# Input rows of a long convolution in sixteen half-array products within one set, modulation vectors broadcast through DRAM, and the second group of channel parameters on GpSimd

## The chip, the cores and the metric

The kernel runs on one core of one Trainium2 chip. The metric is device time in microseconds (us) of a whole run; lower is better. The engines of a core are named as in the profile: PE (TensorE products; PEld its weight loads), DVE (VectorE), ACT (ScalarE), POOL (GpSimd) and SP (SyncE, which issues most DMAs). Each engine works through its own list of instructions in order and waits there on semaphores that other engines and DMAs raise.

## The reference

A block of 2048 tokens by 448 channels goes through two stages, each ahead of a layer norm that is scaled and shifted by vectors made from a condition `c`:

```python
mod = (silu(c) @ w_mod).reshape(1, 6, 1, 448)      # sa, ca, ga, sb, cb, gb
h = layernorm(x) * (1 + ca) + sa
x = x + ga * s4d(h, log_A_real, A_imag, C_real, C_imag, log_dt, D_skip)
h = layernorm(x) * (1 + cb) + sb
x = x + gb * token_mlp(h, w1, b1, w2, b2)          # two matmuls over the token axis, gelu
```

`s4d` makes for each of 448 channels a convolution kernel of 2048 taps, `K = 2 Re sum_n C_n exp(A_n dt l)` over 256 states, and convolves the channel with it (an FFT in the reference).

## The kernel before

The convolution is done as a product of two-step Fourier transforms of length 4096 = 32 x 64 split between PE and the elementwise engines. The program has three parts in a row: the making of `K` with the transform of the input beside it (to about 255 us and on to 380 us), the products and the inverse transform, and the token MLP, which is a stream of PE products to the end.

**Steps and windows.** `K` is made in 56 steps `s` of 16 channels by half of the states. A step (`st_step`) has six ACT functions on 128x512 (`Abs`, `Sin`), four DVE products `E` (L651 to L655) and two POOL products `G` (L649, L650), and PE turns `E` and `G` into `K` (`st_kgen`, `kg`, L676). POOL also makes `w` and `m` (`st_mag2`, L628 and L630), which `E` needs. The phases come from PE (`st_phase`, L601, tiles `xe` and `xg` of PSUM) out of small tiles `lph` that SP loads from `pars`, a table in DRAM. Every eight steps a window (`window(s)`, at s = 0, 8, 16 ...) makes the magnitudes `mag` of the next eight with `Exp` (L612), because ACT's tables for `Exp` and `Sin` have to be swapped; a window has eight parts `e`, and within each PE's products for the next magnitudes come ahead of whatever else PE has to do there.

**Parameters.** Channels come in four groups q of 128. For group 0, `first_chain` turns A, C and dt into logarithms and phases, before step 0, and sends rows to `lex`, `lph` and `pars`. For the groups 1 to 3 a generator (`chain(q)`) does the same with some 36 DVE operations on 128x256; it stops at "logs" until the next window has run `Ln`, `Arctan` and `Exp` for it on ACT. `more(n)` runs n of its steps at fixed places: `pace[s]` in a step, `WPACE` in a part of a window. Its `split` makes a pair `hl` (high and low part; three buffers) which SP stores to `pars`.

**Input side.** `x` (2048x448) is loaded into `xt` by POOL DMAs (`x_load`), DVE takes mean and variance of each of 16 rows of tiles (`u_stats`), `u_norm` normalises them, and `u_rows` does the 32-point step: PE products of `xt` with `wu` into a PSUM tile `pu` (pool `pms`, three buffers), then one DVE product with the vector `mod[1]` (L526) into `yt` (three buffers), then a store of 448 KB to `yu_d` in DRAM. `u_load` reads that back transposed (`yi`), and `u_cols` does the 64-point step, with results `uo` stored to `us_d`. The vectors `mod[0..5]` are made by `modulation(k)`: PE multiplies `w_mod` (loaded by `wm_load`) with a copy of silu(c) in 128 columns (`scb`), so that each result comes out on all 128 partitions, and ACT copies it.

**What sets the order.** PE, ACT, DVE and POOL run in the order in which the code is written: operations that read PSUM are put in the lists `dve` and `act` and emitted by `flush`. SP's order is written order up to step 8 (`first.close()`), and after that it is chosen at build time by a scheduler that knows estimated durations; on the chip SP then goes through that list in order. Each DMA also takes one of eight semaphores per kind of queue in turn, so a DMA is issued only when the one eight places earlier has landed.

Of the kernel before, what the change touches and what calls it, by code (L numbers as in the profile page):

```python
# [11 lines left out]
F32 = mybir.dt.float32  # L12
# [27 lines left out]
def dft_tables():  # L40
# [16 lines left out]
    t["WU"] = np.tile(w1.transpose(1, 2, 0).reshape(32, 64), (4, 1))  # L57
# [45 lines left out]
    t["S2"] = su.reshape(2, 4, 8, 2, 32 * P).transpose(3, 0, 2, 1, 4).reshape(P, 32 * P)  # L103
# [113 lines left out]
def tile_adaln_s4d_mixer(ctx, tc, i, out):  # L217
# [6 lines left out]
    yu_d = dram.tile([2, 32, 2, 8, 4, D], F32, name="yu_d")  # L224
    us_d = dram.tile([2, 32, P, DC], F32, name="us_d")
    v_d = dram.tile([32, P, D], F32, name="v_d")
    x2_d = dram.tile([L, D], F32, name="x2_d")

# [9 lines left out]
    with ExitStack() as es:  # L238
# [27 lines left out]
        def par_load(q):  # L266
            n = min(P, D - P * q)
            raws[q] = {}
            for nm in ("A_C_real", "A_C_imag", "A_log_A_real", "A_A_imag"):
                raws[q][nm] = qp.tile([P, N], F32, tag=nm, name=nm, bufs=2)  # L270
                nc.sync.dma_start(raws[q][nm][0:n], i[nm][P * q : P * q + n])
# [40 lines left out]
        wu = xp.tile([P, 64], F32, name="wu")  # L312
        wms = {}

        def wm_load(k, tile, eng=nc.sync):
            wms[k] = tile
            eng.dma_start(wms[k], i["w_mod"][:, k * D : (k + 1) * D].rearrange("(q p) d -> p q d", p=PP))
# [11 lines left out]
        def wm_slot(k):  # L329
            w = wm0.rearrange("p k d -> p (k d)")[0:PP]  # L330
            return w[:, 4 * D * (k % 4) : 4 * D * (k % 4 + 1)].rearrange("p (q d) -> p q d", q=4)

        late = {
            2: lambda: wm_load(2, wm_slot(2), G),
            3: lambda: wm_load(3, wm_slot(3), G),
            5: lambda: wm_load(0, wm_slot(0), G),
# [4 lines left out]
            9: lambda: nc.sync.dma_start(svt, i["SV"]),  # L343
            10: lambda: [s2_load(0), s2_load(1)],
            11: lambda: [s2_load(2), s2_load(3)],
            12: lambda: wm_load(4, xt[0:PP, 0:4]),
            13: lambda: wm_load(5, xt[0:PP, 4:8]),
# [14 lines left out]

        def chain(q):

# [7 lines left out]
            def split(src, places):  # L372
                hl = qp.tile([P, 2, N], F32R, tag="hl", name="hl", bufs=3)[0:n]
                V.tensor_copy(hl[:, 0], src)
                yield
                tt(hl[:, 1], src, hl[:, 0].bitcast(F32), ALU.subtract)
# [27 lines left out]
            stt(s, t, -80 * math.log(2.0) / 2.0**80, s, ALU.mult, ALU.add)  # L404
            yield
            stt(s, ya, 0.5, s, ALU.mult, ALU.add)
            yield
            ts(s, s, ldt2[0:n, q : q + 1], None, ALU.add)
# [4 lines left out]
            ts(ph, aim, dt4[0:n, q : q + 1], None, ALU.mult)  # L413
            yield
            ts(u, ph, MAGIC, MAGIC, ALU.add, ALU.subtract)
# [942 lines left out]
```

## Time and profile before

| | us |
|---|---|
| median of 3 runs | 725.6 |
| lowest and highest run | 722.94, 727.5 |
| the profiled execution, its own time | 724.45 |
| its span in the profile | 722.7 |
| PE busy in the span | 627.9 (87%) |
| DVE, ACT, POOL busy | 460.3, 438.7, 273.2 |
| granted PE clock, mean | 0.939 |

The page's line of 40 slices (18 us each) reads PE at 0 to 8 tenths in the first slices, between 7 and 9 up to 360 us, and at 9 or more from there to the end; DVE, ACT and POOL are busiest in the first half. A row of the timeline reads: start, duration, engine, line, operation, output<-input, and in brackets the idle time ahead of it on that engine and what ended it. A busy time is no measure of what an engine costs: what counts is whose work the others wait for in a stage.

### The profile page before, as it was taken

To read this page: it belongs to the slowest core of one execution; us is meant where nothing else is said; L and a number is where in the kernel's file an instruction comes from. 1 tells how busy PE (TensorE), PEld (TensorE's weight loads), DVE (VectorE), ACT (ScalarE), POOL (GpSimd) and SP (SyncE) were. 2 spreads that over 40 slices of the span, in tenths; PEclk is the share of its full clock that TensorE was granted. 3 is DMA by queue.
4 is the path that set the end of the run, shared out by engine and by line. 5 is a ranking of instruction groups with operands and counts; after the bars stand their busy time and mean duration, and the time that the engine had idled before them with its cause. 6 is when DMAs were issued, how large, how long until landed. Compare 5 with 4: busy or idle time off the path is not lost. (4 is left out here: it accounts for less than half of the span.)

```text
span 722.7 us, 18269 instructions
## 1 busy us (share of the span) xinstructions
PE 627.9 (87%) x7204; PEld 449.9 (62%) x7204; DVE 460.3 (64%) x891; ACT 438.7 (61%) x849; POOL 273.2 (38%) x342
## 2 busy tenths in 40 slices
PE   0769899969988877888778939999999999999997
PEld 0335344535535545555455607777999999999996
DVE  7579779689779667575776738777722263333441
ACT  5848578887988888979862339778622242222220
POOL 6487438438648867977865600000000000000000
PEclk9988857988999989899999969999999999999999
DMA  6795364277888644444325899993585436655540
GB/s 169 207 189 144 144 195 136 112 234 197 236 225 251 212 84 144 127 128 122 96 82 164 233 274 248 237 224 100 169 230 166 141 99 173 176 164 154 153 140 27
DMA packets 101636, 121.20 MB, mean 168 GB/s; under 512 B 13066, under 2 KB 87422, under 8 KB 101422
## 3 DMA queue, kind: packets, MB, share of 16 engines
q1 hardware_dynamic: 100014, 113.16, 55.4%
q0 software_dynamic: 1536, 6.87, 4.2%
q8 instruction: 57, 0.93, 0.6%
q14 instruction: 29, 0.24, 0.1%
HBM read 84.64 MB, written 34.87 MB: 165 GB/s over the span
## 5 line engine op out<-in xcount | busy, mean ns | idle before, releaser
L202 ACT CAST whi<-w 128x896 fp32r<-128x896 f32 x64 | 59.8, 938 | 135.2 <-PE o L1325 84.7
L649 POOL TENSOR_TENSOR G<-mag,gs 128x512 f32<-128x512 f32 x56 | 71.8, 1282 | 86.5 <-ACT gs L645 86.3
L211 DVE TENSOR_TENSOR wlo<-w,whi 128x896 fp32r<-128x896 f32 x64 | 68.1, 1087 | 43.9 <-ACT whi L202 31.5
L601 PE MATMUL xg<-tab,lph 64*128 64x512 f32 x112 | 68.3, 612 | 21.3 <-ACT xg L647 7.1
L1190 PE MATMUL acc<-h3h,whi 128*128 128x448 f32 x224 | 83.6, 373 | 0.1
L1191 PE MATMUL acc<-h3l,whi 128*128 128x448 f32 x224 | 82.1, 367 | 0.0
L1192 PE MATMUL acc<-h3h,wlo 128*128 128x448 f32 x224 | 81.3, 363 | 0.0
L1325 PE MATMUL o<-ul,whi 128*128 128x448 f32 x224 | 81.3, 363 | 0.0
L1324 PE MATMUL o<-uh,whi 128*128 128x448 f32 x224 | 81.2, 362 | 0.0
L1326 PE MATMUL o<-uh,wlo 128*128 128x448 f32 x224 | 80.6, 360 | 0.0
L601 PE MATMUL xe<-tab,lph 64*128 64x512 f32 x112 | 67.8, 607 | 12.4 <-ACT gs L646 7.0
L676 PEld LDWEIGHTS kg<-E,G 128*32 128x32 f32 x3584 | 57.9, 117 | 29.6 <-issue 14.9
L650 POOL TENSOR_TENSOR G<-mag,gs 128x512 f32<-128x512 f32 x56 | 71.6, 1279 | 0.0
L676 PE MATMUL kg<-E,G 128*32 128x64 f32 x3584 | 67.7, 231 | 1.2 <-POOL G L649 0.5
L651 DVE TENSOR_TENSOR E<-m,xe 128x512 f32<-128x512 f32 x56 | 38.3, 683 | 38.2 <-ACT xe L644 29.8
L1328 DVE SCALAR_TENSOR_TENSOR y<-o,b,mod 128x448 f32<-128x448 f32 x16 | 10.9, 684 | 80.2 <-PE o L1326 80.2
L630 POOL TENSOR_TENSOR m<-mag,w 128x512 f32<-128x512 f32 x56 | 59.8, 1067 | 5.8 <-DVE E L655 1.5
L642 ACT ACTIVATE ab<-xe 128x512 f32<-128x512 f32 x56 | 33.9, 605 | 29.2 <-PE xe L601 17.9
L1190 PEld LDWEIGHTS acc<-h3h,whi 128*128 128x128 f32 x224 | 42.5, 190 | 13.9 <-ACT h L1246 7.0
L601 PE MATMUL xe<-tab,lex 64*128 64x512 f32 x56 | 30.4, 557 | 18.4 <-POOL wm L832 16.7
L612 ACT ACTIVATE mag<-xe 128x512 f32<-128x512 f32 x56 | 34.6, 619 | 16.5 <-PE xg L601 10.3
L1192 PEld LDWEIGHTS acc<-h3h,wlo 128*128 128x128 f32 x224 | 42.3, 189 | 3.0
(231 smaller groups left out, 1467.1 us busy)
## 6 DMA issues: line engine op xcount, KB each, us to landing
w<-in_B_w_dram SPq DMA_DIRECT2D x64, 224.0 KB
w<-in_B_w_dram SPq DMA_DIRECT2D x32, 448.0 KB
yu_d<-yt SPq DMA_DIRECT2D x16, 448.0 KB
yi<-yu_d SPq DMA_DIRECT2D x32, 224.0 KB
us_d<-uo SPq DMA_DIRECT2D x16, 448.0 KB
u<-us_d SPq DMA_DIRECT2D x32, 224.0 KB
v_d<-vt SPq DMA_DIRECT2D x32, 224.0 KB
vt<-v_d SPq DMA_DIRECT2D x16, 448.0 KB
```

What stands on the lines that cost most here:

```text
L202: self.nc.scalar.copy(hi, w)
L211: eng.tensor_tensor(lo, w, hi.bitcast(F32), ALU.subtract)
L601: T.matmul(out[k], lhs[r], rhs[r], start=start, stop=stop)
L649: G.tensor_tensor(Gt[:, 1], mg_, v32(sg), ALU.mult)
L650: G.tensor_tensor(Gt[:, 0], mg_, v32(cg_), ALU.mult)
L676: T.matmul(kgs[g][32 * q : 32 * q + 32, m], Gt[:, c, d], E[:, c, d], start=h == 0 and c == 0 and m == 0, stop=h == 1 and c == 1, skip_grou ...
L1190: nc.tensor.matmul(acc[f], hi[:, fs], h3h[:, r], start=r == 0, stop=False)
L1191: nc.tensor.matmul(acc[f], hi[:, fs], h3l[:, r], start=False, stop=False)
L1192: nc.tensor.matmul(acc[f], lo[:, fs], h3h[:, r], start=False, stop=r == 15)
L1324: nc.tensor.matmul(o, hi[:, ks], uh[kh][:, k], start=kh == 0 and k == 0, stop=False)
L1325: nc.tensor.matmul(o, hi[:, ks], ul[kh][:, k], start=False, stop=False)
L1326: nc.tensor.matmul(o, lo[:, ks], uh[kh][:, k], start=False, stop=kh == 1 and k == 6)
```

## The change

- **`u_rows`.** The matrix `wu` becomes 128x128 with two interleaved blocks, so a product takes 64 rows of `xt` and fills all 128 partitions of a `pu` tile. Two such products, on the two halves of the array, make one row of tiles r: 32 products in place of 64, 16 calls in place of 32. All 16 calls now lie in the window at s = 8 (two for each part e); before they went from that window through the steps 8 to 15 into the window at s = 16. The layout of `yu_d` and of the table `S2` follows. `u_norm` is on DVE for four rows and on ACT for twelve.
- **Modulations.** Three vectors are made at once, each in 32 columns of the array, from `scb` with 32 columns. ACT copies the 96 partitions to `row`, SP stores three rows of it to a new DRAM tensor `mod_d` and loads each back to all partitions. Vectors 0 to 2 are made in steps 3 to 6, 3 to 5 in steps 12 to 15; before, vectors 0, 4 and 5 were made at the start of the windows 8 and 16.
- **Group 1 on GpSimd.** `chain(1)` runs up to "logs" on DVE in window 0, and the rest of it, 32 operations, on POOL in window 8; the five operations with two steps of arithmetic in one instruction (`scalar_tensor_tensor`) become two instructions there. The groups 2 and 3 stay on DVE, mostly in the windows 16 and 24.
- **Loads.** All of `x` and three of the four blocks of `w_mod` are issued by POOL right after `first_chain`, behind a copy (`late0`) that waits for the last row of `lph`; before, POOL issued a quarter of `x` in the middle of `first_chain` and the rest after the steps 0 and 1. The parameters of group 1 are loaded from ACT's queue.
- **`u_cols`** starts at step 10 in place of 17, in pairs.

The core of the diff:

```diff
-    t["WU"] = np.tile(w1.transpose(1, 2, 0).reshape(32, 64), (4, 1))
+    wu = np.zeros((2, 2, 32, 32, 2, 2))
+    for g in range(2):
+        wu[:, g, :, :, :, g] = w1.transpose(1, 2, 0)
+    t["WU"] = wu.reshape(P, P)
...
-        def wm_load(k, tile, eng=nc.sync):
-            wms[k] = tile
-            eng.dma_start(wms[k], i["w_mod"][:, k * D : (k + 1) * D].rearrange("(q p) d -> p q d", p=PP))
+        def wm_load(j, q, tile, eng=nc.sync):
+            wms[j, q] = tile
+            eng.dma_start(tile, i["w_mod"][PP * q : PP * (q + 1), 3 * j * D : 3 * (j + 1) * D])
...
+        def fuse(eng, out, a, c, b, op0, op1):
+            if eng is V:
+                stt(out, a, c, b, op0, op1)
+                return
+            part = a if out is b else out
+            eng.tensor_scalar(part, a, c, None, op0)
+            eng.tensor_tensor(out, part, b, op1)
+
         def chain(q):
+            late_eng = G if q == 1 else V
...
-        def modulation(k, *halves):
-            if 0 in halves:
-                pmods[k] = pms.tile([P, D], F32, tag="ms", name="pm")
-            for h in halves:
-                for q in (2 * h, 2 * h + 1):
-                    T.matmul(pmods[k], scb[:, q], wms[k][:, q], start=q == 0, stop=q == 3)
-            if 1 not in halves:
-                return
-            pm = pmods.pop(k)
-            act.append(lambda: S.activation(mod[k], pm, AF.Copy, bias=1.0 if k in (1, 4) else 0.0))
+        def modulation(j, q):
+            if q == 0:
+                pmods[j] = pms.tile([P, D], F32, tag="ms", name="pm")
+            for k in range(3):
+                r = slice(32 * k, 32 * k + 32)
+                T.matmul(pmods[j][r], scb[:, q], wms[j, q][:, k * D : (k + 1) * D], start=q == 0, stop=q == 3)
...
+            def out():
+                S.copy(row[0:96], pm[0:96])
+                nc.sync.dma_start(mod_d[3 * j : 3 * j + 3], row[0:96:32])
+                for k in range(3 * j, 3 * j + 3):
+                    nc.sync.dma_start(mod[k], mod_d[k : k + 1].to_broadcast([P, D]))
...
+        def u_rows(r):
+            R, o = divmod(r, 2)
+            yt = xp.tile([P, 2, D], F32, tag="yt", name="yt", bufs=3)
+            pm = [pms.tile([P, D], F32, tag="ms", name="pu") for _ in range(2)]
+            for g in range(2):
+                p = slice(64 * g, 64 * g + 64)
+                T.matmul(pm[g], wu[p], xt[p, r], start=True, stop=True)
+
+            def out(g):
+                tt(yt[:, g], pm[g], mod[1], ALU.mult)
+                if g:
+                    nc.sync.dma_start(yu_d[o, :, :, :, R].rearrange("k c a g d -> (k c a) (g d)"), yt.rearrange("p g d -> p (g d)"))
+
+            dve.extend([partial(out, 0), partial(out, 1)])
+            if r + 6 < 16:
+                act.append(partial(u_norm, r + 6))
...
             S.activation(one, one, AF.Ln)
+            par_load(1, nc.scalar)
...
-            x_load(0, 4, G)
...
             hc = split(V, xa)
             direct(hc, lph, 96, 0)
+            G.tensor_copy(late0, lph[0][96:97, 0:1].bitcast(F32))
+            x_load(0, 4, G)
+            x_load(4, 4, G)
+            wm_load(0, 0, wm_slot(0), G)
+            x_load(8, 4, G)
+            wm_load(0, 1, wm_slot(1), G)
+            x_load(12, 4, G)
+            wm_load(0, 2, wm_slot(2), G)
...
             if s == 8:
+                stt(mod[1], mod[1], 1.0, mod[2], ALU.add, ALU.mult)
                 u_scale()
-                u_norm(0)
-                u_norm(1)
-
-            if s in (8, 16):
-                for k in (0,) if s == 8 else (4, 5):
-                    modulation(k, 0, 1)
+                for r in range(4):
+                    u_norm(r)
+                act.extend([partial(u_norm, 4), partial(u_norm, 5)])
...
-                if s in (8, 16):
-                    some(u_rows, rows, (2, 2, 2, 2, 2, 0, 1, 1)[e])
-                elif s == 24 and e != 5:
+                if s == 8:
+                    some(u_rows, rows, 2)
+                elif s in (16, 24) and e in (2, 4, 7):
                     some(u_cols, cols, 1)
...
-        WPACE = [[0] * 8, [0, 5, 4, 4, 4, 4, 4, 4], [0, 5, 4, 4, 4, 4, 4, 4], [2] * 8]
-        pace = [2] * 32
+        WPACE = [[0, 0, 0, 2, 2, 2, 2, 0], [2, 3, 4, 4, 4, 4, 4, 4], [2, 3, 4, 4, 4, 4, 4, 4], [2, 3, 4, 4, 4, 4, 4, 4]]
+        pace = [0] * 8 + [1] * 24
...
-            if 8 <= s < 16 and free:
-                some(u_rows, rows, 2 if s % 2 else 3)
...
-            if 17 <= s < 32 and free:
-                some(u_cols, cols, 2 if s < 24 else 3)
+            if 10 <= s < 32 and s % BATCH != BATCH - 1:
+                some(u_cols, cols, 2 if free and not 11 < s < 16 else 1)
```

Three places show how the order moves. The first is POOL between `first_chain` and step 0. Before (`wm` is here the storage of the first chain's `split`, `m` and `w` belong to step 0):

```order
L832 TENSOR_TENSOR wm_79<-p_186,wm_79 128x256
L466 COPY dsk<-dskr 1x112 x4
L628 TENSOR_TENSOR w<-mag 128x16
L630 TENSOR_TENSOR m_327<-mag,w 128x512
L628 TENSOR_TENSOR w<-mag 128x16
L630 TENSOR_TENSOR m_341<-mag,w 128x512
L649 TENSOR_TENSOR G<-mag,gs 128x512
```

And in the changed kernel:

```order
L852 TENSOR_TENSOR wm_80<-p_188,wm_80 128x256
L928 COPY late_180<-lph_143 1x1
L296 DMA xt<-in_A_u_dram 32x1792 x8
L322 DMA wm_80<-in_w_mod_dram 112x1344
L296 DMA xt<-in_A_u_dram 32x1792 x4
L322 DMA wm_80<-in_w_mod_dram 112x1344
L296 DMA xt<-in_A_u_dram 32x1792 x4
L322 DMA wm_80<-in_w_mod_dram 112x1344
L481 COPY dsk<-dskr 1x112 x4
L647 TENSOR_TENSOR w<-mag 128x16
L649 TENSOR_TENSOR m_357<-mag,w 128x512
```

Nineteen DMA issues of POOL (sixteen of `xt`, three of `wm`) now stand ahead of the first `w` and `m`. By the rule of eight semaphores each from the sixth on waits for the load eight places earlier (the three loads of `tab` at the program's start count too); the last `wm` waits for the tenth load of `xt`.

The second is SP's list in window 8. Before (`hl` and `pars` are the parameters of group 1 from DVE, `yt` and `yu_d` the input rows):

```order
L528 DMA yu_d<-yt 128x896
L378 DMA pars_58<-hl 128x512 x2
L271 DMA A_log_A_real<-in_A_log_A_real_dram 64x256
L528 DMA yu_d<-yt 128x896
L378 DMA pars_58<-hl 128x512
L528 DMA yu_d<-yt 128x896
```

And in the changed kernel, where `hl` comes from POOL:

```order
L391 DMA pars_58<-hl 128x512 x2
L275 DMA A_log_A_real<-in_A_log_A_real_dram 64x256
L606 DMA lex_146<-pars_58 32x256
L548 DMA yu_d<-yt 128x896 x2
L391 DMA pars_58<-hl 128x512 x3
L548 DMA yu_d<-yt 128x896 x2
L391 DMA pars_58<-hl 128x512
L548 DMA yu_d<-yt 128x896 x2
L610 DMA lex_146<-pars_58 64x1x256
L548 DMA yu_d<-yt 128x896 x2
```

Six stores of parameters and sixteen of input rows share the list; the stores of the rows 2 and 3 now stand behind the fifth store of POOL's parameters, and those of 4 and 5 behind the sixth and last.

The third is DVE in the same window. Before (`hl`, `s` and `u` are the chain's, L526 the products of `u_rows`):

```order
L989 TENSOR_TENSOR mod_105<-mod_105,mod_106 128x448
L695 TENSOR_TENSOR ks<-ks,dsk 128x4
L526 TENSOR_TENSOR yt<-pu,mod_105 128x448 x2
L374 CAST hl<-A_log_A_real 128x256
L376 TENSOR_TENSOR hl<-A_log_A_real,hl 128x256
L404 SCALAR_TENSOR_TENSOR s<-t,s 128x256
L406 SCALAR_TENSOR_TENSOR s<-u,s 128x256
L408 TENSOR_SCALAR s<-s,ldt_172 128x256
L998 TENSOR_TENSOR mod_104<-mod_104,mod_106 128x448
L526 TENSOR_TENSOR yt<-pu,mod_105 128x448 x2
```

And in the changed kernel (the `E` rows belong to step 8):

```order
L528 SCALAR_TENSOR_TENSOR nm<-mv,rs 128x16
L532 TENSOR_SCALAR xt<-xt,rs,nm 128x448 x4
L714 TENSOR_TENSOR ks<-ks,dsk 128x4
L546 TENSOR_TENSOR yt<-pu,mod_106 128x448 x8
L714 TENSOR_TENSOR ks<-ks,dsk 128x4
L546 TENSOR_TENSOR yt<-pu,mod_106 128x448 x20
L670 TENSOR_TENSOR E<-m_1007,xe 128x16x32
L671 SCALAR_TENSOR_TENSOR E<-mag,xe 128x16x32
L546 TENSOR_TENSOR yt<-pu,mod_106 128x448 x4
```

Before, operations of the chain of group 1 stood between the products of `u_rows`; now the products of 14 rows follow one another ahead of step 8's first `E`, and the last two rows come after it. Since `yt` has three buffers, the first product of a row also waits for the store of the row three earlier.

161 lines of the change are left out of this document (74 added, 87 removed).

## The prediction, made before the changed kernel was run

> **What bounds the kernel now.** I read the stages first: busy time of each engine between the moments at which POOL starts the `G` of steps 0, 7, 8, 15, 16, 23, 24 and 31.
>
> ```profile
> core 0: us, PE busy (x) PEld busy (x) DVE busy (x) ACT busy (x) POOL busy (x), PEclk, DMA share, GB/s
> 30.30:69.60 39.30, 28.31 (x432) 15.61 (x436) 32.26 (x57) 23.91 (x49) 31.30 (x38) 0.87 0.79 174
> 69.60:102.50 32.90, 29.79 (x320) 12.01 (x308) 23.49 (x57) 21.39 (x41) 10.19 (x12) 0.74 0.52 174
> 102.50:132.80 30.30, 27.93 (x494) 14.20 (x492) 29.47 (x50) 27.56 (x55) 25.63 (x27) 0.78 0.42 142
> 132.80:158.40 25.60, 22.69 (x390) 13.01 (x388) 17.66 (x45) 20.81 (x39) 5.10 (x7) 0.91 0.45 163
> 158.40:187.60 29.20, 25.49 (x436) 13.57 (x440) 27.59 (x44) 24.47 (x51) 25.40 (x26) 0.85 0.79 208
> 187.60:208.90 21.30, 19.79 (x342) 10.06 (x330) 13.23 (x30) 19.22 (x37) 5.38 (x6) 1.00 0.91 260
> 208.90:238.40 29.50, 24.30 (x456) 13.16 (x455) 28.98 (x49) 25.23 (x52) 26.15 (x27) 1.00 0.79 229
> 380.00:722.70 342.70, 323.42 (x1738) 276.84 (x1738) 173.77 (x350) 133.64 (x246) 21.38 (x48) 0.98 0.63 172
> ```
>
> The change lies ahead of step 32; what comes after keeps its order and, in the last row, is PE's. So what the stages up to 238 us lose or gain reaches the end one for one. In a stage of seven steps DVE, ACT and POOL are all nearly full. Next, POOL's timeline:
>
> ```profile
> 16.52 1.59 POOL L466 COPY dsk<-dskr 1x112 f32<-1x112 f32 x4
> 30.34 1.27 POOL L649 TENSOR_TENSOR G<-mag,gs 128x512 f32<-128x512 f32 x1 [8.49 <-ACT gs L645]
> 31.57 1.26 POOL L650 TENSOR_TENSOR G<-mag,gs 128x512 f32<-128x512 f32 x1
> 32.78 2.00 POOL L292 DMA_DIRECT2D xt<-in_A_u_dram  x4
> 34.79 0.26 POOL L628 TENSOR_TENSOR w<-mag 128x16 f32<-128x16 f32 x1
> 35.13 1.05 POOL L630 TENSOR_TENSOR m<-mag,w 128x512 f32<-128x512 f32 x1
> 41.98 0.77 POOL L317 DMA_DIRECT2D wm<-in_w_mod_dram  x1
> 69.59 1.29 POOL L649 TENSOR_TENSOR G<-mag,gs 128x512 f32<-128x512 f32 x1 [1.32 <-ACT gs L645]
> 102.53 1.28 POOL L649 TENSOR_TENSOR G<-mag,gs 128x512 f32<-128x512 f32 x1 [18.33 <-ACT gs L645]
> ```
>
> A step costs POOL two `G` (2.5 us) and one `w`, `m` pair (1.35): 3.85 us, the floor of a step. From the first to the eighth `G` 39.25 us pass where seven floors are 27; in the window POOL is idle for 18 us.
>
> **Part 1, the front.** The rest now goes to loads: DVE waits for `xt`, PE for a late `lph`.
>
> ```profile
> 45.57 0.63 DVE L492 BATCH_NORM_STATS2 st<-xt 128x6 f32<-128x448 f32 x1 [5.12 <-DMA xt<-in_A_u_dram]
> 51.60 0.76 PE L601 MATMUL xg<-tab,lph 64*128 64x512 f32 x1 [7.11 <-issue]
> ```
>
> The change removes these waits and DVE's chain from steps 0 to 7, but puts POOL's issues ahead of the first `m`. Where they start and how fast they land:
>
> ```profile
> 21.10 1.25 SPq L842 DMA_DIRECT2D lph<-wm  x2
> 22.40 2.04 SPq L846 DMA_DIRECT2D pars<-wm  x4
> 25.40 0.76 PE L601 MATMUL xe<-tab,lph 64*128 64x512 f32 x1
> 40.00:45.00 5.00, 4.48 (x76) 2.30 (x73) 0.44 (x1) 2.50 (x5) 4.89 (x7) 1.00 1.00 225
> xt<-in_A_u_dram POOLq DMA_DIRECT2D x8, 224.0 KB, 7.7
> ```
>
> The last `lph` is issued at 21.8 and used by 25.4: POOL's copy `late0` passes at about 25. Its last issue waits for the tenth load of `xt`: ten times 224 KB and one `w_mod` block of 588 KB (112 x 1344 x 4), 2.9 MB, beside about half of the six parameter stores of 256 KB still under way and small `lph` loads, 1.0 MB. At 225 GB/s (a DMA share of 1.00) this is 17.3 us: POOL is free at 42.5, and after one more issue (0.75), the `dsk` copies (1.6) and two `w`, `m` pairs (2.7) the first `G` starts at 47.5. From there to the eighth: seven pairs of `G` (17.5), six of `w`, `m` (8.0), one issue (0.75): 73.7, against 69.59. **+4.** Ends: without the semaphore waits sixteen issues of 0.5 and three of 0.75 are 10.2 us, 7 less, of which DVE's own work of 3.9 us a step returns some: -3. At 170 GB/s (the whole stage had 174): 23 us, +9. ACT's four new issues (some 1.8 us ahead of `first_chain`'s logarithms) are hidden by POOL's hold, and would cost at most that without it.
>
> **Part 2, window 8.** A call of `u_rows` was four PE passes and eight passes took 1.77 us (second row below), 28 us for all 128; of the new products on 64 rows half as many passes are needed, and two of them share the array as the 64-row `xe` and `xg` do, so about 14 us are left. DVE loses the chain. PE was not waiting for itself, though. What counts is the way of a row: `pu`, DVE, `yt`, SP, DRAM.
>
> ```profile
> 75.10 0.49 ACT L456 ACTIVATE A_log_A_real<-A_log_A_real,ldt 128x256 f32<-128x256 f32 x1
> 77.42 1.77 PE L523 MATMUL pu<-xt,wu 32*64 32x448 f32 x8 [0.74 <-POOL xt L510]
> 79.11 1.16 DVE L526 TENSOR_TENSOR yt<-pu,mod 128x448 f32<-128x448 f32 x2 [2.26 <-PE pu L523]
> 100.07 1.28 ACT L644 ACT_TABLE_LOAD   x1
> 12.37 0.29 DVE L831 CAST wm<-s 128x256 fp32r<-128x256 f32 x1
> 13.52 0.52 POOL L831 CAST wm<-ph 128x256 fp32r<-128x256 f32 x1 [2.54 <-DVE ph L890]
> 14.12 0.72 POOL L832 TENSOR_TENSOR wm<-ph,wm 128x256 fp32r<-128x256 f32 x1
> L510 POOL TENSOR_SCALAR xt<-xt,rs,nm x6: 704/730/1127, 76.4 to 81.5; 128x448 f32<-128x448 f32 x6
> 151.38 0.32 SPq L528 DMA_DIRECT2D yu_d<-yt  x1
> 156.01 1.30 SPq L546 DMA_DIRECT2D yi<-yu_d  x2
> SPq L546 <- DMA yu_d<-yt: 0.8, 1, 0.8
> ```
>
> Let t0 be the end of the `Exp` of group 1 (75.6 in the first row); step 8's first `G` (102.53) then came 26.9 us after t0. POOL's chain starts at t0. Its 32 operations are 5 casts at 0.60, 13 two-input products at 0.78 (both with the 0.08 us gaps between dependent ones) and 14 one-input ones at 0.53 (0.73 at 448 elements, scaled): 20.6 us, and two `w`, `m` pairs 2.75.
>
> So the fifth store's pair is ready at t0+15.7 and the last at t0+23.5, and SP, in order, holds rows 2, 3 until the one and 4, 5 until the other. A row's store takes 4.6 us from issue to landing (151.38 to 156.01, where `yi` waited for exactly this). Row 7 needs row 4's buffer: 23.5 + 0.5 + 4.6 = t0+28.6. DVE needs 1.15 us a row: rows 8, 9 end at 30.9 and 32.0. Row 10 waits for row 7's store (29.7 + 4.7 = 34.4), row 12 for row 9's (36.7). PE stands in order behind DVE with its three `pu` buffers, so step 8's phases follow row 12's first product, at 37.5; phases (1.4), two `Abs` (1.0), table load (1.3) and two `Sin` (1.0) put `G` at t0+42: **+15.** Behind PE wait ACT's `Exp` and so the whole window. Ends: with raw durations and a store of 3 us that never blocks again, row 7 is at t0+24.5, five more rows 5.8, then 4.7: t0+35, +8; with 6 us a store under the load of its neighbours, +18.
>
> `row` adds one ACT copy of 0.5. The way of `mod` through DRAM is two DMAs one after the other (the small one to `lph` above took at most 3.6 us, so up to 7) and delays DVE's first rows: copied near 71, `mod[1]` is back near 78, and DVE's scaling and four norms (some 3 us) stand behind it, where PE had its first input at 77.42 before. The rows wait for SP later anyway, which hides these 3 to 4 us; without SP's hold they would count.
>
> By the Trainium skill, DMA: Bandwidth & Descriptors, section Anatomy of one DMA, a DMA costs 2.0 us and its bytes over 436 GB/s: 3.05 us for 448 KB, where this trace has 4.6; the sum below would then be 3 us less, 733.5. The same skill, GPSIMD Engine Reference, section Engine selection, calls one-input operations on GpSimd roughly line-rate and two-input ones twice as slow as on VectorE; for the cast this trace has 0.52 against 0.29 on DVE, so it does not agree there. With the 19 one-input operations at DVE's rate, row 7 would come 4.4 us earlier: 732.
>
> **Part 3, steps 8 to 15.** Without the input rows DVE has 2.4 us of `E`, one chain operation and a `uo`; POOL's floor makes 27 us of 30.2. But rows 14 and 15 stand between step 8's `E`, wait for stores again, and `u_cols` at step 10 waits on PE for `yi`, two DMA trips after row 15. **-0.5**, ends -3 and +2.
>
> **Part 4, windows 16 and 24, steps 24 to 31.**
>
> ```profile
> 137.07 6.28 PE L479 MATMUL pm<-xt,scb 112*128 112x448 f32 x16
> 143.83 0.59 ACT L612 ACTIVATE mag<-xe 128x512 f32<-128x512 f32 x1
> 146.83 0.28 DVE L374 CAST hl<-A_log_A_real 128x256 fp32r<-128x256 f32 x1
> 192.26 1.02 PE L555 MATMUL pu<-yi,s 128*128 128x448 f32 x2
> ```
>
> In window 16 the modulations hold PE for 6.3 us, ACT's third `Exp` starts only at 143.8 and DVE's chain at 146.8, 7 us after its own `Exp`. With the products gone to the steps before, ACT runs through: 16 `Exp` of 0.48 and 2.5 us of copies, table load and `Sin` end near 153 in place of 158: **-4.5** (-6 to -2). Window 24 loses four of its seven `u_cols` (1.0 us each on PE), but gains 12 chain operations on DVE, 10 us in all: **-1** (-3 to +1). Steps 24 to 31 have 5 `u_cols` left: **-1.5** (-3 to 0). In steps 12 to 15 the modulations' three products share the array (0.9 us for a block), within the 3.85.
>
> **Sum**: 4 + 15 + 0.5 - 0.5 - 4.5 - 1 - 1.5 = +12. The profiled execution took 724.45 (span 722.7): 736.5, 10.9 above the median of the runs shown, which is itself 1.15 above that execution.
>
> **The rivals.**
> - A, faster: the window is set by DVE's work alone. If POOL's chain kept within some 12 us (0.35 an operation) the parameter stores would be ahead of the rows, and if stores landed in 3 us the ring of three would turn in 1.15 us a row: 16 rows are 18.4, of which 14 stand ahead of step 8, with a start at t0+5 and 4.7 for phases and `Sin`: t0+25. Then -2 in place of +15: 719.5; together with a front of -3, 712.5. For it: DVE's busy time really falls. Against it: the casts and products above, all at 0.5 or more, and the 4.6 us.
> - B, about the same: the window stalls, but POOL's issues are not held. -3 in place of +4: 729.5. Against it speaks the order of semaphores; for it, that the first quarter of `xt` landed early in the run.
> - C, slower still: loads at 170 GB/s and stores of 6 us: +9 and +18, 744.5, and more if step 10 waits for `yi`.
>
> **How the numbers follow.** Forecast 0.47, A 0.27 (a third of it with both gains), B 0.13, C 0.13. A measurement tells about 1% (7.3 us) from no change. Faster by over 1% (under 718.3) is two thirds of A, whose 719.5 lies beside the bound: 0.18. Within 1% (up to 732.9) are the rest of A, B and 0.08 of the forecast's lower end: 0.30, and slower is what is left: 0.52. The range 716 to 748 leaves out A with both gains and the upper part of C; the forecast's own, by the ends of the two large terms taken one at a time, is 730 to 743.
>
> **What would show it.** Right: first `G` near 47 with POOL's sequencer held on DMA issues from 28 on; in window 8 SP waiting for POOL's `hl`, DVE for `yu_d` stores, PE for DVE, and `G` of step 8 some 42 us after the `Exp`; window 16 some 5 us shorter. Wrong: a first `G` near 35 or a window 8 of at most 27 us after t0, with SP never behind; then A or B holds.

## The result, and the profile after

The changed kernel takes 748.9 us (median of 4 runs, 746.81 to 752.78), the kernel before beside it 726.55: a ratio of 1.0279, interval 1.0229 to 1.0329. The forecast was slower, at 736.5 with a range to 748: the direction came, at about twice the size. The profiled execution took 748.71, its span is 746.9, 24.2 more than before. A later run of the same kernel (`after_2`) had its profiled execution in the slow state (1007 us at a granted clock of 0.56), so no stage is read from that one. Busy times by stage, cut where POOL starts the first `G` of steps 0, 7, 8, 15, 16, 23, 24 and 31, as in the prediction's first view:

```profile
core 0: us, PE busy (x) PEld busy (x) DVE busy (x) ACT busy (x) POOL busy (x), PEclk, DMA share, GB/s
47.90:73.80 25.90, 22.44 (x458) 12.83 (x458) 24.15 (x51) 20.66 (x41) 25.41 (x28) 0.85 0.40 97
73.80:130.40 56.60, 35.02 (x276) 20.42 (x276) 25.13 (x48) 27.11 (x49) 28.78 (x39) 0.67 0.48 176
130.40:162.80 32.40, 26.87 (x466) 14.75 (x466) 29.73 (x46) 24.98 (x51) 26.58 (x27) 0.84 0.89 230
162.80:185.30 22.50, 20.91 (x376) 11.33 (x376) 15.43 (x37) 19.59 (x38) 5.49 (x7) 0.92 0.62 189
185.30:216.00 30.70, 26.50 (x440) 14.18 (x444) 28.34 (x44) 25.47 (x53) 26.92 (x28) 0.89 0.84 238
216.00:238.50 22.50, 20.26 (x330) 10.90 (x318) 17.59 (x41) 18.51 (x35) 5.39 (x6) 0.77 0.61 168
238.50:263.80 25.30, 20.25 (x505) 12.74 (x504) 21.28 (x35) 23.86 (x49) 24.80 (x26) 0.93 0.55 168
```

Nearly all of it is the second row. Window 8, from step 7's first `G` to step 8's, lasts 56.6 us where it lasted 32.9; in it PE, the busiest engine, works for 35. The front is 4.2 us later, the steps 24 to 31 are 4.1 shorter, the other stages change by 1 to 3 us each way, and from step 32 to the end nothing changes (467.2 us against 468.1). POOL's timeline in the front and in the window:

```profile
29.34 0.54 POOL L322 DMA_DIRECT2D wm<-in_w_mod_dram  x1 [1.76 <-DMA xt<-in_A_u_dram]
41.15 0.49 POOL L296 DMA_DIRECT2D xt<-in_A_u_dram  x1 [3.10 <-DMA wm<-in_w_mod_dram]
47.91 1.27 POOL L668 TENSOR_TENSOR G<-mag,gs 128x512 f32<-128x512 f32 x1
79.80 0.40 POOL L387 CAST hl<-A_log_A_real 128x256 fp32r<-128x256 f32 x1 [3.50 <-ACT A_log_A_real L471]
93.85 0.41 POOL L434 TENSOR_SCALAR u<-ph 128x256 f32<-128x256 f32 x1
94.34 0.86 POOL L436 TENSOR_SCALAR u<-u 128x256 f32<-128x256 f32 x1
107.62 0.73 POOL L389 TENSOR_TENSOR hl<-xa,hl 128x256 fp32r<-128x256 f32 x1
130.45 1.28 POOL L668 TENSOR_TENSOR G<-mag,gs 128x512 f32<-128x512 f32 x1 [22.10 <-ACT gs L664]
```

The chain runs from 79.80 to 108.35, and then POOL is idle for 22.1 us. What happens meanwhile stands on SP and DVE (three rows of SP, then four of DVE; the brackets hold the idle time ahead and what ended it):

```profile
90.65 7.80 SPq L391 DMA_DIRECT2D pars<-hl  x3
108.79 0.87 SPq L548 DMA_DIRECT2D yu_d<-yt  x2
110.58 2.58 SPq L548 DMA_DIRECT2D yu_d<-yt  x2
101.39 1.76 DVE L546 TENSOR_TENSOR yt<-pu,mod 128x448 f32<-128x448 f32 x3 [4.47 <-DMA yu_d<-yt]
111.66 1.92 DVE L546 TENSOR_TENSOR yt<-pu,mod 128x448 f32<-128x448 f32 x3 [7.07 <-DMA yu_d<-yt]
116.92 1.16 DVE L546 TENSOR_TENSOR yt<-pu,mod 128x448 f32<-128x448 f32 x2 [2.06 <-DMA yu_d<-yt]
121.40 2.12 DVE L546 TENSOR_TENSOR yt<-pu,mod 128x448 f32<-128x448 f32 x3 [3.33 <-PE pu L543]
```

SP stands at the parameter stores until POOL has made each pair. Rows 4 and 5 were ready in `yt` and could be stored only at 108.79, behind the last pair; only 2.87 us later, when row 4's store had landed, did DVE have a buffer for row 7. This is the chain that the prediction described. Row 6's store, issued at 110.58, took longer: DVE could start row 9 in its buffer only at 116.92, 6.3 us after the issue.

### The profile page after: what moved, and what is told of

Same layout as the page of the kernel before. It is cut to its first block, busy times and chain, and to the rows that moved or that the text cites. A ratio compares the mean times of both kernels' runs of the same rounds, so it can differ in the third digit from the quotient of the medians.

```text
span 746.9 us, 18209 instructions
## 1 busy us (share of the span) xinstructions
PE 621.5 (83%) x7140; PEld 454.2 (61%) x7140; DVE 452.6 (61%) x867; ACT 438.9 (59%) x847; POOL 295.3 (40%) x376
## 5 line engine op out<-in xcount | busy, mean ns | idle before, releaser
L214 DVE TENSOR_TENSOR wlo<-w,whi 128x896 fp32r<-128x896 f32 x64 | 68.0, 1086 | 42.9 <-ACT whi L205 30.5
L620 PE MATMUL xe<-tab,lph 64*128 64x512 f32 x112 | 65.3, 584 | 28.1 <-POOL m L649 19.4
L695 PEld LDWEIGHTS kg<-E,G 128*32 128x32 f32 x3584 | 61.9, 123 | 30.1 <-issue 14.0
L620 PE MATMUL xg<-tab,lph 64*128 64x512 f32 x112 | 66.1, 592 | 11.3 <-DVE E L674 6.8
L695 PE MATMUL kg<-E,G 128*32 128x64 f32 x3584 | 72.0, 240 | 3.3 <-ACT ks L709 2.1
L620 PEld LDWEIGHTS xe<-tab,lph 64*128 64x128 f32 x112 | 22.8, 204 | 44.5 <-POOL m L649 19.8
L631 ACT ACTIVATE mag<-xe 128x512 f32<-128x512 f32 x56 | 34.7, 620 | 23.7 <-PE pu L543 20.0
L620 PE MATMUL xe<-tab,lex 64*128 64x512 f32 x56 | 33.8, 623 | 17.2 <-DMA lex<-wm 13.5
L664 ACT ACTIVATE gs<-xg 128x512 f32<-128x512 f32 x56 | 34.1, 609 | 21.5 <-POOL G L668 21.5
```

The source lines that it names most:

```text
L214: eng.tensor_tensor(lo, w, hi.bitcast(F32), ALU.subtract)
L620: T.matmul(out[k], lhs[r], rhs[r], start=start, stop=stop)
L695: T.matmul(kgs[g][32 * q : 32 * q + 32, m], Gt[:, c, d], E[:, c, d], start=h == 0 and c == 0 and m == 0, stop=h == 1 and c == 1, skip_grou ...
```

## The experiments

The table has every kernel's stages and its ratio to the kernel before on the same chip. G(n) is the start of the first `G` of step n in the kernel's POOL timeline; window 8 is the time from G(7) to G(8), and steps 8-15 that from G(8) to G(15). The stages of a row are those of one profiled execution. One look at window 8 isn't exact: `e_dve` and `e_polo` have the same program up to step 8 and read 41.6 and 45.7 us.

| kernel | G(7) at | window 8 | steps 8-15 | G(15) to G(32) | ratio, 95% interval |
|---|---|---|---|---|---|
| before | 69.6 | 32.9 | 30.2 | 121.8 | 1 |
| the change | 73.8 | 56.6 | 32.4 | 116.9 | 1.0279 (1.0229-1.0329) |
| e_dve | 73.7 | 41.6 | 30.9 | 117.9 | 1.0152 (1.0112-1.0192) |
| e_forms | 75.7 | 50.6 | 31.9 | 116.0 | 1.0262 (1.0230-1.0294) |
| e_pst | 74.8 | 45.8 | 30.5 | 117.3 | 1.0224 (1.0196-1.0253) |
| e_fp | 75.1 | 47.8 | 31.6 | 114.3 | 1.0131 (1.0086-1.0176) |
| e_polo | 73.7 | 45.7 | 32.0 | 116.8 | 1.0121 (1.0073-1.0169) |
| e_front | 75.6 | 57.1 | 32.3 | 116.7 | 1.0354 (1.0316-1.0391) |
| f_pool | 75.2 | 44.0 | 32.1 | 117.7 | 1.0127 (1.0049-1.0206) |
| f_sync | 68.0 | 47.8 | 31.9 | 116.1 | 1.0103 (1.0066-1.0139) |
| e_mod1 | 74.3 | 44.1 | 30.6 | 117.5 | 1.0099 (1.0061-1.0137) |
| g_dve | 73.7 | 30.3 | 43.8 | 128.8 | 1.0275 (1.0196-1.0353) |
| g_pool | 74.7 | 34.5 | 46.0 | 125.2 | 1.0289 (1.0205-1.0373) |
| g_mod1 | 75.2 | 29.9 | 45.1 | 128.0 | 1.0231 (1.0153-1.0310) |
| g_sync | 66.5 | 33.8 | 45.5 | 126.4 | 1.0182 (1.0090-1.0273) |
| h_dve | 74.4 | 32.0 | 33.2 | 118.6 | 0.9965 (0.9931-0.9999) |
| h_sync | 70.2 | 35.3 | 33.2 | 120.5 | 0.9949 (0.9910-0.9988) |
| h_pool | 75.0 | 31.6 | 33.2 | 119.2 | 1.0016 (0.9978-1.0053) |
| h_mod1 | 74.6 | 29.9 | 33.3 | 116.1 | 0.9979 (0.9941-1.0017) |

### The chain on POOL and the hold on SP

```diff
-            late_eng = G if q == 1 else V
+            late_eng = V                     # e_dve
```

> The chain of the second group goes back to DVE; all else of the change stays. Hold theory (POOL's slow chain keeps SP's parameter stores late, SP holds the row stores behind them, the ring of three stops DVE and so PE): SP never stands for POOL, the window from G(7) to G(8) falls from 56.6 us to about 44 (some 9.5 us of chain come back to DVE beside 16 rows of 1.15), and the time to about 736. Row theory (the rows' own way, a store of some 3 us with a ring of three and PE in order, sets the window whatever SP does): at least 52 us, 745 or more.

```diff
-                    nc.sync.dma_start(pars[q][v, k, 0:n], hl.bitcast(F32))
+                    (G if q == 1 else nc.sync).dma_start(pars[q][v, k, 0:n], hl.bitcast(F32))   # e_pst
```

> The chain stays on POOL, but its six parameter stores are issued by POOL itself, right behind the operation that makes each pair, in place of SP. Hold theory: SP's row stores no longer stand behind POOL; POOL pays some 4 us for issuing, which nobody waits for, and G(8) comes 35 to 38 us after the Exp of group 1 in place of 50.7: about 735. Row theory: window 8 stays at 52 us or more, 745 or more.

```diff
+        def lone(eng, out, a, c, op):        # e_forms: each one-input operation but L444, L448
+            if eng is V:
+                return ts(out, a, c, None, op)
+            c, d = (c, 0.0) if op is ALU.mult else (1.0, c)
+            eng.tensor_scalar(out, a, c, d, ALU.mult, ALU.add)
```

> On POOL alone, each one-input operation of the chain but two is written as a multiply-add (times 1 or plus 0 where one part was missing; the two roundings become two such operations), the form that took 0.41 us where the others took 0.85 to 1.11. Form theory: those operations take 0.41, the chain falls from 28.5 us to about 24, the last pair and with it G(8) come some 4.4 us earlier: about 744.5. Contention theory (POOL's one-input operations are slow because DVE and the transfers are at SBUF meanwhile): they stay near 0.9, and the time stays within 1 us of 749. Row theory: the chain is shorter, the time is not.

Window 8 of `e_dve`, and of `e_polo` with the same program there (the columns are those of the first view):

```profile
73.70:115.30 41.60, 29.04 (x276) 14.86 (x276) 31.48 (x75) 27.17 (x49) 5.12 (x7) 0.88 0.64 238
73.70:119.40 45.70, 32.01 (x276) 16.95 (x276) 31.48 (x75) 27.24 (x49) 5.20 (x7) 0.77 0.59 219
```

DVE has 6.4 us more to do than in the change, and the window is 11 to 15 us shorter, as the hold theory had it (44). With POOL's own stores 45.8 us were left, more than the 41 to 44 that it had asked (G(8) came 39.8 us after the `Exp`, not 35 to 38), and 738.4 us rather than 735. The forms behave as expected; the same two operations that stand above with 0.41 and 0.86 us read in `e_forms`:

```profile
94.00 0.40 POOL L446 TENSOR_SCALAR u<-ph 128x256 f32<-128x256 f32 x1
94.49 0.40 POOL L378 TENSOR_SCALAR u<-u 128x256 f32<-128x256 f32 x1
97.92 1.10 POOL L456 TENSOR_SCALAR u<-A_C_real 128x256 f32<-128x256 f32 x1
```

The third row is one of the two that kept their form. The chain took 24.8 us, G(8) came 44.6 us after the `Exp` of its group in place of 50.7; but the ratio doesn't tell `e_forms` from the change. Nor does it tell `e_pst` (1.0196 to 1.0253 against 1.0229 to 1.0329), so what the hold and the forms are worth each by itself rests on single looks at window 8; `e_dve` does lie below the change. Both cures together, beside the changed kernel on one chip:

> The chain stays on POOL, with the multiply-add forms of e_forms and POOL's own stores of e_pst. If hold and slow forms are the whole price of POOL's chain: as good as the chain on DVE or better (DVE has 9.5 us less in the window), window 8 at 38 to 42 us, 1.2 % above the kernel before. If the ring of three and the rows' stores set the window once SP is free (row theory, in part): at 44 to 46 as in e_pst, whatever POOL's speed, and 1.8 to 2.2 % above.

> The changed kernel itself, beside the next three on one chip. If the low clock in its window 8 (0.67) was of that one look: window 8 at 50 to 54 us and a ratio near the lower end of the interval (1.023). If it comes of the window's own stalls, window 8 is again within 2 us of 56.6 with a clock below 0.72.

The change gave 1.0263 (1.0206 to 1.0320), much as the first time, and what its window 8 owes to the low clock stays open; `e_fp` gave 1.0131 (1.0086 to 1.0176): hold and forms are worth about 1.3%, 9.6 us, and with both gone the chain on POOL is no worse than on DVE. The window, though, stayed at 47.8, so the row theory holds in part. `e_fp`'s DVE still waits for row stores, although SP no longer holds them behind POOL's pairs:

```profile
102.42 1.16 DVE L558 TENSOR_TENSOR yt<-pu,mod 128x448 f32<-128x448 f32 x2 [3.82 <-DMA yu_d<-yt]
```

### The two operations on modulations

```diff
-                G.tensor_tensor(mod[0], mod[0], mod[2], ALU.mult)     # step 8
+                tt(mod[0], mod[0], mod[2], ALU.mult)
-                G.tensor_scalar(mod[4], mod[4], 1.0, None, ALU.add)   # step 20
+                ts(mod[4], mod[4], 1.0, None, ALU.add)
```

> The chain on DVE as in e_dve, and the two operations on modulations that the change gave to POOL at steps 8 and 20 (mod 0 times mod 2, 1.13 to 1.33 us; mod 4 plus 1, 1.51 us) on DVE. The prediction did not price them. If POOL's floor sets those steps, steps 8 to 15 and 16 to 23 shorten by 1.1 and 1.5 us, from 30.9 to 29.8 and from 30.1 to 28.6, and the time falls by 2.5 us or 0.35 %. If DVE is as full as POOL there, nothing changes (within 0.5 us).

Steps 8 to 15 took 32.0 us and steps 16 to 23 31.4, no less than `e_dve`'s 30.9 and 30.1. POOL's floor alone doesn't set them; this reason for the change's +2.2 and +1.4 there falls, and the +1.4 stays open.

### The front

`e_front` puts the loads back; `f_pool` and `f_sync` spread them in order of use (`feed[s]()` behind step s), from POOL or from SP, with the chain on DVE. The cut is that of `f_pool`.

```diff
-            x_load(0, 4, G) ... wm_load(0, 2, wm_slot(2), G)     # behind late0
+            x_load(0, 4, G)                                      # ahead of Square, as before
+        feed = {
+            0: lambda: x_load(4, 4, G),                          # f_sync: nc.sync in place of G
+            1: lambda: [wm_load(0, q, wm_slot(q), G) for q in (0, 1)],
+            2: lambda: [wm_load(0, q, wm_slot(q), G) for q in (2, 3)],
+            3: lambda: x_load(8, 4, G),
+            4: lambda: x_load(12, 4, G),
+        }
```

> The loads of x and of the modulations' weights go back to their places of before (x behind the first directs and in steps 0 and 1, the weights in steps 2 to 5, all from POOL), the rest of the change stays. If POOL, held on its issues, is what the front lost: G(0) near 30 to 33, G(7) near 69 to 70 in place of 73.8, about 745. If something else holds the front (DVE's statistics, or a later w_mod that PE waits for): G(7) stays at 73 or later, and the time at 748 or more.

> The chain on DVE as in e_dve, and the early loads undone, but unlike e_front spread in the order in which they are used: x 0 to 3 at the place of before, x 4 to 7, w_mod blocks 0 and 1, blocks 2 and 3, x 8 to 11, x 12 to 15 behind steps 0 to 4, all issued by POOL. If POOL's hold made the front +4, and e_front only turned it into PE's wait for w_mod behind x: G(0) near 33 and G(7) at 66 to 69 in place of 73.7, the time 5 to 7 us below e_dve (0.5 to 0.8 % above the kernel before). If the volume of loads is what the front takes (6 MB at 225 GB/s from 25 on end at 52 wherever they stand): G(7) at 73 again.

> As f_pool, but x 4 to 15 and the w_mod blocks are issued by SP, which has no work there but the parameter loads. POOL then pays no issue (16 of 0.5 and 4 of 0.58 us, 10 us in all, 8 of them behind steps 0 to 4): if POOL's sequencer is the front's bound, G(7) comes at 60 to 64, 4 to 8 us before f_pool's, and the time is at or below the kernel before. If the transfers or DVE's statistics decide, G(7) stands within 1 us of f_pool's; if SP's own waits hold the parameter loads of the next groups, PE waits for lph or lex and G(7) comes later than f_pool's.

`e_front` started G(0) at 32.92, as expected, and G(7) at 75.6, as its rival had it. The 15 us moved to PE, which stood in order at a block of `w_mod` queued behind `x`, with `kg` and the phases behind it:

```profile
61.20 0.97 PE L498 MATMUL pm<-wm,scb 112*32 112x448 f32 x3 [15.21 <-DMA wm<-in_w_mod_dram]
```

In `f_pool` DVE waited 13.6 us for `x` rows 8 and up, and G(7) stood at 75.2. Only `f_sync`, whose POOL issues nothing after the first quarter, reached 68.0, short of the 60 to 64 expected: DVE stood 5.3 and 4.6 us ahead of the statistics of `x` rows 8 and 12. Its window 8 was 47.8, so 1.0103 overlaps `e_dve`'s 1.0152. The hold on POOL was real, but freeing POOL bought nothing as long as another engine waited in order for the same 6 MB.

### The way of the modulations through DRAM

```diff
-            if 2 < s < 7:
-                modulation(0, s - 3)
+            if 1 < s < 6:
+                modulation(0, s - 2)                              # e_mod1, g_mod1, h_mod1
```

> The chain on DVE as in e_dve, and the four modulation blocks for the input rows one step earlier (behind steps 2 to 5, not 3 to 6), so that the way through DRAM starts some 3.8 us earlier. The prediction said that this way (DVE waited 4.6 us for it in e_dve) is hidden behind SP's hold and counts without the hold. If so: DVE's wait falls to about 1 us, the window from G(7) to G(8) from 41.6 to about 38, and the time from 1.5 % to about 1.0 % above the kernel before. If DVE's total work in the window, or the rows' stores, decide: the window stays within 1 us of 41.6.

DVE's wait for `mod` falls from 4.6 us to 0.8. The window is 44.1 us, neither the 38 nor the 41.6 of the two theories; `e_polo`, at the same clock of 0.77, had 45.7, so the gain is 1.6 us. `g_mod1` gained 0.4 and `h_mod1` 2.1 (29.9 against 32.0), with ratios that can't be told from their partners'.

> As g_dve, with the first three modulations one step earlier (as in e_mod1). With fewer rows in the window the start of the first counts more: DVE's wait of 4.6 us for mod goes, window 8 is 3 to 4 us shorter than g_dve's, and the time falls by 0.4 to 0.5 %, to about that of the kernel before. If DVE's and PE's later work sets the end of the window as in e_mod1 (which gained 1.6 us at the same clock): 1 to 2 us, 0.2 %.

> As h_dve, with the first modulations one step earlier, so that DVE's wait of 4.8 us for mod goes. If that wait stands at the end of window 8's path: 28 to 30 us in place of 32.0, a ratio of 0.991 to 0.994. If ACT's and PE's work in the window cover it (e_mod1 gained 1.6 us, g_mod1 0.4): within 1 us, and no difference from 0.9965 that can be told.

### The rows

```diff
-                    some(u_rows, rows, 2)                         # window 8, each part e
+                    some(u_rows, rows, (1, 1, 1, 1, 1, 0, 1, 1)[e])
+            if 8 <= s < 16 and free:
+                some(u_rows, rows, 2 if s % 2 else 1)             # g_*: steps 8 to 14
```

> The half-array products stay, but their 16 rows are not all in window 8: 7 there, the other 9 behind steps 8 to 14 as the kernel before had its products; with them the column products go back behind step 17, the second three modulations to steps 18 to 21. The chain is on DVE. Cover theory: a row costs DVE 1.15 us; in window 8 nothing covers it, in steps 8 to 15 POOL's 3.85 us a step do. Then window 8 falls by some 10 us from the 41.6 and 45.7 that two kernels with this window showed, to 31 to 35, steps 8 to 15 stay at 31 to 32, steps 16 to 31 lose 2 to 4, and the time is 0.2 to 0.6 % above the kernel before, in place of 1.2 to 1.5. If the way of mod through DRAM, the chain or PE's clock set the window: 40 us or more, and the time at 1.2 % or above.

> The same spreading of the rows, with the chain on POOL and its stores on SP as in the change. Of the 7 rows of the window six stand ahead of step 8's E. Hold theory: SP still stands for POOL's pairs, but only the sixth row needs a buffer whose store was held (row 2 behind the fifth store, 18.4 us after the Exp of group 1): window 8 at 35 to 38 in place of 56.6, then set by POOL's own 28.6 us, and the time 0.5 to 0.9 % above the kernel before. If the slow chain alone made the loss (POOL late for its own G): the window stays over 45.

> As g_dve, with the loads of f_sync (x 4 to 15 and w_mod from SP behind steps 0 to 4). f_sync showed G(7) at 67.95 in place of 73.66, but lost it in window 8, where DVE's 36.5 us of work stood with a clock of 0.78. With 10 us fewer of rows there, G(7) at 68 again, and the gain of 5 us reaches the end: 0.5 to 0.7 % below g_dve, at or below the kernel before. If the statistics that are then late (DVE waits for x 8 to 15) only move into window 8: the same time as g_dve.

Window 8 did what the cover theory asked, 30.3 us (34.5 with the chain on POOL), but the steps after it took 43.8 to 46.0, with two of 11 and 10 us, and G(15) to G(32) grew by 8 to 12 us for a reason that was not looked for. The total was no better than the change. In `g_sync` G(7) at 66.5 left G(8) 3.8 us ahead of `g_dve`'s, and the ratios overlap. A step with two rows makes four `pu` tiles for three PSUM buffers, and DVE's products come only with the next step's `flush`; PE stands at the fourth, with `kg` behind it (`g_dve`):

```profile
126.12 1.11 PE L544 MATMUL pu<-xt,wu 64*128 64x448 f32 x1 [4.11 <-DVE yt L547]
```

So the spreading had a fault of its own, which the next kernels mend:

```diff
-                    some(u_rows, rows, (1, 1, 1, 1, 1, 0, 1, 1)[e])
+                    some(u_rows, rows, 1)
-            if 8 <= s < 16 and free:
-                some(u_rows, rows, 2 if s % 2 else 1)
+            if 8 <= s < 16:
+                some(u_rows, rows, 1)
...
+            wm_load(1, q, xt[0:PP, 3 * q : 3 * q + 3].rearrange("p r d -> p (r d)"))   # modulations in steps 12 to 15
...
+                up.tile([P, 2, 2, DC], F32, tag="uo", name="uo", bufs=6)
```

> As g_dve, but with one row in each of the eight steps of window 8 and one behind each of the steps 8 to 15 (never more than two of the three PSUM buffers of a step), the second modulations from the places of x rows that are done with, in steps 12 to 15 as in the change, and six buffers for the column products' rows. Cover theory: window 8 at 31 to 35, steps 8 to 15 at 30 to 32 with no step over 7 us, the front still +4: 0.0 to 0.5 % above the kernel before. If the rows cost in the steps what they cost in the window (no cover there): steps 8 to 15 at 38 or more, 1.2 % or above.

> As h_dve, with the loads of x 4 to 15 and of w_mod from SP behind steps 0 to 4, as in f_sync and g_sync, where G(7) came at 67.95 and 66.48 in place of 73.7. With window 8 at 31 to 35 the front's 5 to 7 us reach the end: 0.4 to 0.9 % below h_dve, that is at or below the kernel before (a ratio of 0.992 to 1.000). If not, window 8 grows by what the front gains.

> The rows as in h_dve, the chain on POOL in its cheap forms (24.8 us from its first cast to its last subtraction in e_forms), its stores on SP as in the change. If the hold on SP is what made POOL's chain dear: only a row whose buffer waits for a store behind POOL's pairs is late, and seven rows in the window need few of them, so window 8 is bound by POOL's own 24.8 us behind the Exp, 31 to 35 us as in h_dve, and the time is within 0.4 % of h_dve's 0.9965. If the hold works with one row a step too: window 8 at 37 or more, 0.5 % or more above the kernel before.

Window 8, steps 8 to 15 and steps 24 to 31 of `h_dve`, then the front and window 8 of `h_sync`, and last, beside the second row, steps 8 to 15 of `e_dve`:

```profile
74.40:106.40 32.00, 22.85 (x256) 13.28 (x256) 23.20 (x61) 24.92 (x46) 5.15 (x8) 0.73 0.65 220
106.40:139.60 33.20, 29.66 (x504) 16.96 (x507) 30.96 (x52) 25.70 (x52) 26.36 (x27) 0.85 0.53 173
211.20:240.90 29.70, 26.11 (x458) 13.89 (x456) 24.50 (x41) 25.26 (x53) 25.32 (x26) 0.94 0.86 248
33.70:70.20 36.50, 24.61 (x457) 13.93 (x457) 21.77 (x44) 22.23 (x45) 24.89 (x27) 0.72 0.73 160
70.20:105.50 35.30, 24.54 (x257) 14.07 (x257) 28.24 (x68) 25.38 (x47) 5.44 (x6) 0.71 0.62 200
115.30:146.20 30.90, 26.31 (x466) 14.59 (x466) 29.51 (x46) 24.78 (x51) 26.79 (x28) 0.89 0.93 236
```

With nine of the 16 rows out of the way (eight in the steps, the eighth of the window behind step 8's `E`), window 8 is 32.0 us where it was 41.6 and 45.7, and steps 8 to 15 grow only from 30.9 and 32.0 to 33.2. That POOL's `G` and `m` cover the rows there, as the cover theory has it, is not shown: DVE is the busier engine (31.0 us against 26.4), and it has only 1.5 us more to do than in `e_dve`, although its row products go from 4 to 14 (2.3 to 8.1 us), because four column products (2.6 us) have left these steps and other operations took less time. The column products come back behind step 17, and no run moves the rows alone. The whole is 0.9965 against 1.0121 and 1.0152. `h_sync` gained 4.2 us in the front and gave 3.3 back in window 8, since DVE's statistics are late by then; it cannot be told from `h_dve`. Both lie just under the kernel before, 0.35 and 0.5%, with intervals that end at 0.9999 and 0.9988, while those of `h_mod1` and `h_pool` include 1: the products, the modulations and the loads of the change with the rows spread are a small gain at best.

`h_pool` answers the last question. POOL's chain, with the cheap forms and SP's hold still there, ends just ahead of its own `G`, and DVE waits for stores as in the change:

```profile
105.92 0.62 DVE L555 TENSOR_TENSOR yt<-pu,mod 128x448 f32<-128x448 f32 x1 [4.08 <-DMA yu_d<-yt]
105.50 0.73 POOL L401 TENSOR_TENSOR hl<-xa,hl 128x256 fp32r<-128x256 f32 x1
106.66 1.28 POOL L677 TENSOR_TENSOR G<-mag,gs 128x512 f32<-128x512 f32 x1 [0.43 <-ACT gs L673]
```

But the window is 31.6 us, and the ratio of 1.0016 overlaps that of `h_dve`. Window 8 in four kernels: 56.6 us with sixteen rows and the chain on POOL as in the change, 41.6 and 45.7 with sixteen rows and the chain on DVE, 34.5 with seven rows and the chain on POOL (`g_pool`), 30.3 with seven rows and the chain on DVE (`g_dve`). So POOL's chain and SP's order cost 11 to 15 us where sixteen rows stand in the window and need their buffers back, and some 4 where seven do.

## Why the prediction was right and wrong

**What bounds the kernel.** Right: what was lost ahead of step 32 reached the end, 25.2 us there and 24.2 at the end.

**Front, +4.** Right, by its own steps: first `G` at 47.91 (47.5 forecast), G(7) at 73.81 (73.7), POOL held at its issues until 43.9. That undoing it would give this back was only implied, and `e_front` shows otherwise (G(7) at 75.6).

**Window 8, +15 and 0.5 for the copy: the step that failed, in size.** Measured +23.7, which is 8.2 of the 12.2 us by which the time was missed; G(8) came 50.7 us after t0, the end of the `Exp` (79.7), not 42. The mechanism (POOL's pairs, SP's order, three `yt` buffers, PE in order) is in the rows above, and `e_dve`, `e_pst` and `e_fp` take it apart. The mis-sized term is "14 one-input ones at 0.53": they took 12.5 us, 0.89 each, in place of 7.4, and so the last pair came at t0+28.6 in place of 23.5. The price was scaled from the only large one-input row on POOL, the old `u_norm`, which is a multiply-add; the chain has two of that form. The profile of the kernel before had a row that spoke for the other, a negation of 64 elements in each partition with a copy of the same size beside it (groups by line: busy us, mean ns of one):

```profile
L759 POOL TENSOR_SCALAR bt<-yk 128x64 f32<-128x64 f32 x15 | 5.5, 367 | 0.0
L760 POOL COPY bt<-yk 128x64 f32<-128x64 f32 x15 | 3.5, 234 | 0.0
```

A single multiply took 1.6 times as long as the copy. The upper end of the range was drawn from slow stores alone, and no end held a slower POOL. Row 4's store was priced too high instead: 2.87 us, not 4.6. So row 7 came 3.3 us later than forecast, and `e_forms`, with the cheap forms, had G(8) at t0+44.6. By the Trainium skill, DMA: Bandwidth & Descriptors, section Anatomy of one DMA, 448 KB take 3.05 us, an estimate from its formula, which it gives for DMAs issued by GpSimd, while these stores are SP's. The trace agrees at row 4 (2.87 us) and does not at row 6 (6.3 us).

The other 5.4 us lie behind row 7: from there to G(8) it took 18.8 us and not 13.4. Row 9 waited for row 6's store, which took 6.3 us where the sum had 4.7, and row 10 did not wait for a store but for PE (3.33 us at 121.40), which had 64 products `y` (L733) to make between 116.05 and 119.58 that the sum did not have. The granted clock in the window was 0.67: the same 276 products kept PE busy for 35.0 us there and for 29.0 in `e_dve` at 0.88. How much of the delay the clock made was not shown apart from the stalls; `h_dve`'s window took 32.0 us at 0.73.

What the prediction did not see is which edit weighs most. It priced the chain and took the place of the rows as given. The runs show the place of the rows as the larger choice in window 8: with the change's chain left on POOL, seven rows in place of sixteen made 34.5 us out of 56.6; with all the rows left, the chain on DVE made 41.6 and 45.7. The prediction's sentence on steps 8 to 15, that POOL's floor makes 27 of their 30.2 us, so that they gain little by losing the rows, was the other half of this, but its reason is not shown: `e_polo` took work off POOL there and gained nothing.

**`mod` through DRAM.** "Without SP's hold they would count": hardly. 0.4 to 2.1 us in three pairs of single looks, and nothing that the times tell.

**Steps 8 to 15, -0.5 (-3 to +2).** +2.2, just out. The first step took 6.8 us against 4.1, with rows 14 and 15 between its products, as named; `h_dve` and `e_dve` have 5.1 and 5.8 there, `e_polo` again 6.8.

**Windows 16 and 24, steps 24 to 31: -7.** -3.1, +1.3 and -4.1 make -5.9. Each of the last two lies outside its own bounds; that together they are -2.8 where -2.5 was said is luck. With the column products back behind step 17, steps 24 to 31 take 29.7 us (`h_dve`) in place of 25.3; but `e_pst`, with the early start, read 30.0 there and 18.7 in window 24, so what the early start is worth was not settled. Steps 16 to 23, which had no term, cost +1.4.

**The rivals.** A, the window set by DVE alone, did not come, but names what is left when the hold is gone: `e_dve`'s DVE is busy for 31.5 of 41.6 us. B fails by POOL's rows at 29 to 43. C had the size (744.5) but not the way: its front of +9 did not come, of its stores at 6 us one did (row 6's), and the slow one-input operations were not in it.

## What to carry to other kernels

Before work is gathered into one place, ask of both places what else runs there: eight rows less made window 8 some 10 to 14 us shorter, and the steps that took them in, from which the column products had left, 1 to 2 us longer. A queue that works in order turns a slow producer into a wait for whatever stands behind it; what it holds matters most where buffers run out, so count the buffers against the hold. And price an operation by a row of the same form, not only of the same engine and shape: a small row of the right form would have been nearer than a large one of another.

## What the hardware showed that was not expected

- POOL's one-input arithmetic on 128x256 depends on its form: multiply-add 0.40 to 0.48 us (`e_forms`; the longer ones with a scalar per partition), a single multiply, add or subtract 0.85 to 1.11 (the change), other pairs (add and subtract, compare and subtract) 1.07 to 1.10. Two multiply-adds at 0.40 are cheaper than one add-subtract at 1.08. By the Trainium skill, GPSIMD Engine Reference, section Engine selection, one-input operations are roughly line-rate there. Beside the 0.28 to 0.35 us of the same operations on DVE in `e_dve` the multiply-add comes within 1.5 times of that, and the other forms take 2.7 to 3.9 times as long, so the trace agrees for one form only.
- A store of a pair issued by POOL itself (`e_pst`) costs POOL 0.30 us of waiting for its own last result and some 0.6 of issue, together more than a two-input operation (0.73).
- A store of the same 448 KB let its waiter go on after 2.87 us (row 4) and after 6.3 us (row 6) within one window of the changed kernel.
- The granted PE clock in one and the same stretch of program was 0.88 in one execution (`e_dve`) and 0.77 in another (`e_polo`), with 4.1 us between them; a single look at a window is worth no more than that.
